# A linear-attention and GLU block on one core: squares of four more x tiles on ScalarE, their rows loaded earlier, and a new order

## The chip, the cores and the metric
The kernel runs on one core of a Trainium2 chip. The core has a matrix engine (TensorE, PE in the profile), VectorE (DVE), ScalarE (ACT), GpSimd (POOL) and a queue that here only issues DMAs (SyncE, SP). The metric is the device time of one execution in microseconds. The kernel before takes 280.59 us, the median of three runs (280.55 to 281.14).

## The reference
```python
x = A_x                                            # 1 x 2048 x 640, bf16
h = x + A(layernorm(x))
out = h + B(layernorm(h))
# A: qkv = x @ wqkv, 32 heads of 20; pq = q @ w_phi, pk = k @ w_phi (20 x 20 a head)
phi_q = concat(softmax(pq), softmax(-pq))          # 40 features a head, phi_k likewise
kv = phi_k^T v ;  z = sum over the sequence of phi_k
o = (phi_q kv) / (phi_q z + 1e-6) ;  A = o @ wo
# B: (x @ w_gate) * (x @ w_up) @ w_down            # 640 -> 1536 -> 640
```

## The kernel before
The 2048 rows of x are 16 tiles of 128. The 640 columns are five chunks of 128. PSUM is cut into four buffers of two banks each; nearly every step on TensorE takes one buffer and holds it until another engine has read it.

**The stages.** First the weights are prepared: `w_phi` is spread into a block-diagonal band `Phi` (masked by `G`, on VectorE for chunks 0 to 2, on GpSimd for 3 and 4), and the query and key parts of `wqkv` are turned, centred and multiplied by it, so that one matrix takes x straight to pq or pk. The key weights are turned on TensorE at the start (`wk_rounds`, units wk and x0 to x4). The query weights are loaded by the unit lwq, turned by DMAs (units t0 to t4), and centred row block by row block (`wq_means`: the means in unit wm, then units wq0 to wq4, line 739 on VectorE for 0, 2 and 4, line 736 on ScalarE for 1 and 3). The five rounds y0 to y4 (`wq_round`) then read all five centred blocks and write one chunk of the final weights each. The value weights are centred by units c0 to c4 after their sums (unit wv).

Then come the layer-norm statistics of x, in five batches (`stats`, units s0, s2, s4, s8, s12; the last three of four tiles). In the form with `act` false TensorE multiplies each transposed tile by itself and a column of ones (129 columns), and VectorE takes the diagonal by a product with the identity (line 617). In the form with `act` true, chosen by `ST_ACT`, TensorE multiplies by one column of ones only, and ScalarE squares the rows of x as they lie in `x_all` and sums them (`act_sum`, line 565). On GpSimd a chain of five to seven small operations makes 1/std from them (lines 622 to 633).

For each tile t there are a key step (k: ten matmuls of 320 columns; VectorE's largest absolute value, line 820, and its product `nb`, line 823; two exponentials on ScalarE, line 827), its normalisation (K: VectorE's sum over each head, line 838, and reciprocal, line 840; GpSimd's product of 1280 columns, line 841), a value step (v: ten matmuls, one scaled copy on ScalarE) and a query step (q and Q, like k and K but with lines 860 to 871). When the keys are done, sixteen steps A0 to A14 build kv in one PSUM buffer, and VectorE copies it, masked, to `KVsb` (line 907). Then, per block of four tiles, come the attention output (n), its projection (h), the gate and up products (f, named by block, chunk and first tile) and the down product (d, e).

**What sets the order.** Each operation belongs to a unit. `ORDER` holds for each engine a list of unit names; the n-th mention of a name is the n-th operation of that unit on that engine. Each engine runs strictly by its list. Semaphore waits follow from the data; a planner (`place`) with an assumed duration `t` for each operation only decides which of several equal buffers an operation takes. An `at` of a load is an assumed landing time for the same planner. All transposing DMAs of x (units lT4 to lT15, and four inside "in") and plain loads stand on SP's list, and at most eight transposing DMAs are under way.

`ones`, `ident`, `G`, `Gk`, the column of ones behind each x tile (`R_xone`) and ones columns of `vaug` are written by GpSimd at the start, in the order of the code.

Of the kernel before, what the change touches and what calls it, by code (L numbers as in the profile page):

```python
# [7 lines left out]
ACT = mybir.ActivationFunctionType  # L8
# [3 lines left out]
P = 128  # L12
S = 2048
D = 640
NT = S // P
NC = D // P
H = 32
DH = 20
# [11 lines left out]
DF = 2 * DH  # L30
NQ = 2 * NC
HQ = [P * c // DF for c in range(NQ)]
SL = 4
# [8 lines left out]
SC = 175.0 / 128.0  # L42
# [6 lines left out]

BATCH = [(0, 2), (2, 2), (4, 4), (8, 4), (12, 4)]  # L50

ST_ACT = (12,)

# [1 line left out]

ORDER = {
# [14 lines left out]
    "DVE":  # L73
# [12 lines left out]
    "ACT":  # L86
# [9 lines left out]
    "POOL":  # L96
# [10 lines left out]
}  # L107
# [270 lines left out]
def _build(ctx, nc, A_x, A_wqkv, A_w_phi, A_wo, B_w_gate, B_w_up, B_w_down, out):  # L378
    g = Prog(nc, ctx)
# [9 lines left out]
    xT = sb([P, NT, NC, XW], BF16, "xT")  # L389
# [8 lines left out]
    Wrows = sb([P, NC, DH], BF16, "Wrows")  # L398
    G = sb([P, NC, H], BF16, "G")
    Gk = sb([P, NC, SL], BF16, "Gk")  # L400
# [17 lines left out]
    mhalf = sb([P, 1], FP32, "mhalf")  # L418
    mone = sb([P, 1], FP32, "mone")
# [32 lines left out]
    R_Wnat, R_WT, R_Phi = regs(NC), [regs(NC), regs((NRAW + 1) * NC)], regs(NC)  # L452
# [13 lines left out]
    def load(out_, in_, wr, mb, eng="SP", at=0.0):  # L466
        return g.op(eng, lambda e: e.dma_start(out_, in_), wr=wr, dma=("w", 8), t=0.5, lat=0.4 if at else 1.9, size=mb / 0.38, at=at)  # L467
# [45 lines left out]

    U("in")
    load_wnat(1, (3, 5), "ACT", at=4.3)
    load(Wrows[:, :, :], A_w_phi.rearrange("h d f -> (h d) f").rearrange("(a p) f -> p a f", p=P), [R_Wrows], 0.03, eng="ACT", at=5.5)
    load_wnat(1, (0, 1), at=2.9)
    load_wnat(1, (1, 3), at=5.05)
    load_xT(0, 5.35)
# [6 lines left out]
    def pool_op(f, t, **k):  # L526
        return g.op("POOL", f, t=t, **k)
# [6 lines left out]

    def affine(reg, out_, pattern, base, mult):
        pool_op(lambda e: e.affine_select(out=out_, in_=out_, compare_op=ALU.is_ge, fill=0.0,
                                          base=base, pattern=pattern, channel_multiplier=mult), 0.17, rd=[reg], wr=[reg])

    pool_op(lambda e: e.memset(G[:, :, :], 1.0), 0.23, wr=R_G)
    for c in range(NC):  # L540
        affine(R_G[c], G[:, c, :], [[-DH, H]], P * c, 1)
    for c in range(NC):
        affine(R_G[c], G[:, c, :], [[DH, H]], DH - 1 - P * c, -1)
    pool_op(lambda e: e.memset(Gk[:, :, :], 1.0), 0.15, wr=[R_Gk])
    affine(R_Gk, Gk[:, :, :], [[P - 3 * DF, NC], [-DF, SL]], 0, 1)
    affine(R_Gk, Gk[:, :, :], [[3 * DF - P, NC], [DF, SL]], DF - 1, -1)
    for a in range(NC):
        lo, hi = CH[a]
        n = hi - lo + 1

        def phi_op(e, a=a, lo=lo, hi=hi, n=n):
            return e.tensor_tensor(out=Phi[:, a, 0:DH * n].rearrange("p (h f) -> p h f", f=DH),  # L552
                                   in0=Wrows[:, a, :].unsqueeze(1).to_broadcast([P, n, DH]),
                                   in1=G[:, a, lo:hi + 1].unsqueeze(2).to_broadcast([P, n, DH]), op=ALU.mult)
        g.op("DVE" if a < 3 else "POOL", phi_op, t=0.22 if a < 3 else 0.45, rd=[R_Wrows, R_G[a]], wr=[R_Phi[a]])
    pool_op(lambda e: e.memset(xT[:, :, :, P:P + 1], SC / D), 0.25, wr=[R_xone])
    pool_op(lambda e: e.memset(mhalf[:, :], -0.5), 0.1, wr=[R_const])
    pool_op(lambda e: e.memset(mone[:, :], -1.0), 0.1, app=[R_const])
    for b4 in range(NB):
        pool_op(lambda e, b4=b4: e.memset(vaug[:, 4 * b4:4 * b4 + 4, :, DH:E21], 1.0), 0.6, wr=R_vaug[4 * b4:4 * b4 + 4])  # L560

# [556 lines left out]
```

## Time and profile before
| | |
|---|---|
| median of the runs | 280.59 us |
| the profiled execution | 280.5 us |
| its span | 278.8 us |
| PE busy | 273.6 us |
| DVE busy | 166.2 us |
| ACT busy | 135.3 us |
| POOL busy | 107.3 us |
| granted TensorE clock | 0.999 |

In a row of the timeline the first number is the start in microseconds from the span's start, the second the time that the merged group took, then engine, line, operation, output and inputs, shape and count; in brackets stands the idle time before it and what ended it. Spans of neighbouring instructions on one engine overlap by up to a tenth of a microsecond, and for TensorE by more, so that a step is read from start to start. In a row of groups, the busy time and the mean in nanoseconds of one instruction stand behind the bar. In a row of waits the numbers are the total, the count and, where there is a third, the longest. Time between landing and issue of a DMA is the last number of its row. The profile shows lines of the kernel; operations in helpers such as `mms` (line 572) all carry one line.

### The profile page before, as it was taken

How to read it: one execution, taken by the hardware profiler on the slowest of the kernel's cores; microseconds unless marked ns; L12 is line 12 of the kernel's file. 1: busy time of each engine (PE TensorE's matmuls, PEld its weight loads, DVE VectorE, ACT ScalarE, POOL GpSimd, SP SyncE). 2: the span in 40 equal slices, each digit the busy share in tenths (PEclk: the TensorE clock that was granted, in tenths of full speed). 3: DMA queues.
4: the chain of work that ended last, by engine and by line, in shares of the span. 5: the costliest groups of instructions: out<-in, count | busy, mean ns of one | idle time of the engine just before them, and what ended most of it. 6: DMA issues, size and time to landing. Idle time of an engine off the chain costs nothing.

```text
span 278.8 us, 5485 instructions
## 1 busy us (share of the span) xinstructions
PE 273.6 (98%) x2227; PEld 186.8 (67%) x2239; DVE 166.2 (60%) x314; ACT 135.3 (49%) x229; POOL 107.3 (38%) x158
## 2 busy tenths in 40 slices
PE   8999999999999999999999999999999999999995
PEld 8777777778878788877656555776454444447773
DVE  1999999999999976578445745413250223324011
ACT  3469989999657455323664423113254314340132
POOL 6446799999732240061230912241200000250152
PEclk9999999999999999999999999999999999999999
DMA  7998984068165549558644031447312000000112
GB/s 198 274 143 185 126 275 156 6 151 316 26 73 119 96 93 290 138 94 211 74 101 91 24 70 28 118 94 96 94 27 23 0 0 2 0 24 26 47 47 71
DMA packets 65192, 28.06 MB, mean 101 GB/s; under 512 B 55696, under 2 KB 63888, under 8 KB 65168
## 3 DMA queue, kind: packets, MB, share of 16 engines
q1 hardware_dynamic: 64240, 27.37, 43.7%
q10 hardware_dynamic: 928, 0.35, 0.5%
q8 instruction: 17, 0.28, 0.5%
q14 instruction: 7, 0.06, 0.1%
HBM read 11.82 MB, written 2.62 MB: 52 GB/s over the span
## 4 chain that ended last, share of the span: by engine, by line
PE 95%; DMA 2%; DVE 1%; issue 0%; SPq 0%
PE ps L572 95%; DMA phiqT<-in_A_wqkv_dram 2%; PE ps L482 0%; DVE outb L1024 0%; DVE phiqT L717 0%; PE ps L661 0%; DVE Phi L552 0%; DVE KVsb L907 0%; SPq L467 0%; DVE nmean L690 0%; DVE KVsb L910 0%; DVE sm L613 0%; DVE nb L823 0%
## 5 line engine op out<-in xcount | busy, mean ns | idle before, releaser
L572 PE MATMUL ps<-phik,Wgu 128*128 128x512 bf16 (+1 forms) x589 | 105.9, 336 | 0.6
L572 PEld LDWEIGHTS ps<-phik,Wgu 128*128 128x128 bf16 x600 | 58.2, 98 | 43.5 <-DVE phik L983 1.8
L572 PE MATMUL ps<-Wp,xT 128*128 128x320 bf16 x480 | 68.6, 299 | 0.0
L983 DVE TENSOR_TENSOR phik<-ps,gate 128x512 bf16<-128x512 f32 (+1 forms) x60 | 33.8, 575 | 56.0 <-PE ps L572 51.2
L572 PE MATMUL ps<-vaug,phik 128*128 128x320 bf16 (+3 forms) x543 | 59.8, 270 | 0.1
L981 ACT ACTIVATE gate<-ps 128x512 bf16<-128x512 f32 (+1 forms) x60 | 29.8, 511 | 58.8 <-PE ps L572 43.3
L572 PEld LDWEIGHTS ps<-Wp,xT 128*128 128x128 bf16 x480 | 46.0, 98 | 17.9 <-ACT phik L827 0.5
L572 PEld LDWEIGHTS ps<-vaug,phik 128*128 128x128 bf16 x544 | 43.6, 97 | 15.6
L999 POOL TENSOR_TENSOR outb<-t,x_all 128x640 bf16<-128x640 f32 x12 | 16.8, 1396 | 58.0 <-ACT t L996 49.9
L841 POOL TENSOR_TENSOR phik<-phik,Rk 128x1280 bf16<-128x1280 bf16 x16 | 37.6, 2364 | 2.3 <-DVE Rk L840 2.0
L996 ACT ACTIVATE t<-ps,mh,rs 128x640 f32<-128x640 f32 x12 | 10.6, 883 | 37.8 <-PE ps L572 37.8
L820 DVE TENSOR_REDUCE ps<-ps 128x1 f32<-128x640 f32 x32 | 26.2, 818 | 1.5 <-PE ps L572 1.0
L860 DVE TENSOR_REDUCE Sq<-eq 128x64 f32<-128x1280 bf16 x16 | 23.6, 1473 | 2.7 <-ACT eq L827 2.7
L827 ACT ACTIVATE eq<-ps,nb,rs 128x640 bf16<-128x640 f32 x16 | 14.2, 885 | 20.2 <-DVE nb L823 12.3
L966 POOL TENSOR_SCALAR vpe<-shc 128x1 f32<-128x1 f32 x16 | 3.0, 190 | 52.9 <-ACT junk L565 51.9
L838 DVE TENSOR_REDUCE Ssum<-phik 128x64 f32<-128x1280 bf16 x16 | 23.4, 1471 | 0.0
L871 POOL TENSOR_TENSOR eq<-eq,rq 128x640 bf16<-128x640 bf16 x16 | 20.2, 1269 | 0.8
L866 POOL TENSOR_TENSOR rq<-Sq,rq 128x32 f32<-128x32 f32 x16 | 4.0, 254 | 39.9 <-DVE rq L865 39.9
L565 ACT ACTIVATE junk<-x_all 128x640 bf16<-128x640 bf16 x20 | 14.6, 732 | 4.4 <-DVE x_all L960 4.4
L827 ACT ACTIVATE phik<-ps,nb,rs 128x640 bf16<-128x640 f32 x16 | 14.1, 884 | 2.6 <-DVE nb L823 1.9
L941 DVE RECIPROCAL rden<-ps 128x32 f32<-128x32 f32 (+1 forms) x18 | 5.6, 323 | 14.6 <-PE ps L572 14.6
L827 ACT ACTIVATE phik<-ps,nb,nrs 128x640 bf16<-128x640 f32 x16 | 14.2, 885 | 0.0
(86 smaller groups left out, 245.1 us busy)
## 6 DMA issues: line engine op xcount, KB each, us to landing
x_all<-in_A_x_dram SPq DMA_DIRECT2D x4, 640.0 KB, 5.5
out_dram<-outb SPq DMA_DIRECT2D x15, 160.0 KB, 1.8
Wgu<-in_B_w_up_dram SPq DMA_DIRECT2D x1, 1920.0 KB, 7.9
Wgu<-in_B_w_gate_dram SPq DMA_DIRECT2D x1, 1920.0 KB, 10.2
vaug<-in_B_w_down_dram SPq DMA_DIRECT2D x1, 1920.0 KB, 8.6
Wp<-in_A_wqkv_dram SPq DMA_DIRECT2D x1, 800.0 KB, 5.0
phiqT<-in_A_wqkv_dram SPq DMA_DIRECT2D x1, 800.0 KB, 6.3
Wo<-in_A_wo_dram SPq DMA_DIRECT2D x1, 800.0 KB, 9.5
```

Source lines behind the costliest of these rows:

```text
L565: g.op("ACT", lambda e: e.activation(out=junk[:, v.i, :], in_=in_, func=func, accum_out=acc), rd=rd, wr=wr, use=[v], t=0.73, lat=0.97)
L572: ins = e.matmul(o_, lhsT=l_, rhs=r_, start=s_, stop=p_, skip_group_check=True)
L820: g.op("DVE", lambda e: e.tensor_reduce(out=mx(), in_=PS[v.i][:, :, 0:HALF], axis=AX.XY, op=ALU.max, apply_absolute_value=True, negate=Tru ...
L827: g.op("ACT", lambda e, s=s, sc=sc: e.activation(out=signed(dst(), s), in_=PS[v.i][:, :, 0:HALF].rearrange("p b (h f) -> p b h f", f=DH), ...
L838: g.op("DVE", lambda e: e.tensor_reduce(out=Ssum[:, vs.i, :], in_=x, axis=AX.X, op=ALU.add), rd=R_phik[t], wr=vs.R, use=[vs], t=1.39, lat=1.5)
L841: g.op("POOL", lambda e: e.tensor_tensor(out=x, in0=x, in1=Rk[:, vr.i, :].unsqueeze(2).to_broadcast([P, 2 * H, DH]), op=ALU.mult), rd=vr.R ...
L860: g.op("DVE", lambda e: e.tensor_reduce(out=Sq[:, vs.i, :], in_=eq[:, b.i, :].rearrange("p (g f) -> p g f", f=DH), axis=AX.X, op=ALU.add), ...
L871: return e.tensor_tensor(out=x, in0=x, in1=rq[:, vr.i, :].unsqueeze(2).to_broadcast([P, H, DH]), op=ALU.mult)
L981: g.op("ACT", lambda e: e.activation(out=gate[:, vg.i, 0:P * n], in_=PS[v.i][:, 0, 0:P * n], func=ACT.Copy), rd=[v.R[0]], wr=vg.R, use=[v, ...
L983: g.op("DVE", lambda e: e.tensor_tensor(out=hhT[:, hb, ft, sl], in0=PS[v.i][:, 1, 0:P * n], in1=gate[:, vg.i, 0:P * n], op=ALU.mult), rd=[ ...
L996: g.op("ACT", lambda e: e.activation(out=t32[:, v3.i, :].rearrange("p (b n) -> p b n", b=2), in_=PS[v.i][:, :, 0:HALF], func=ACT.Identity, ...
L999: g.op("POOL", lambda e: e.tensor_tensor(out=outb[:, vo.i, :], in0=t32[:, v3.i, :], in1=x_all[:, t, :], op=ALU.add), rd=v3.R + [R_h[t]], w ...
```

## The change
- `ST_ACT` becomes (8, 12): tiles 8 to 11 take the form with squares on ScalarE. Their rows (`x_all`, unit lx2, 640 KB) move on SP from the middle of the kernel to the first place behind the loads of unit "in", which end with transposed tiles 2 and 3 (tiles 0 to 3).
- On GpSimd the column of ones behind each x tile, and the two small constants, are written earlier, the column ahead of `G`. The ten selects that shape `G` by chunks of 32 columns become two over all 160 columns.
- The lists of all five engines are new up to the middle of the first GLU block; from "f0.5.0 n7" on they are the same but for single names. On SP the query weights go behind tiles 4, 6, 5, 10 and 7, both GLU weights are loaded ahead of Wo, where one of them came later. On TensorE keys and values of more tiles come ahead of the rounds y and the queries q.
- Some of the planner's durations differ. They do no work on the chip, beyond the choice of buffers.

```diff
-ST_ACT = (12,)
+ST_ACT = (8, 12)
 "PE":
-  warm wk*9 s0 wk s0 x1 x1 x3 wv wv x2 x0 x0 s2 s2 x4 k0*5 k3 k2 wm k1 v1 s4*4
-  k6 k4 v5 v0 k7 y3 v7 v4 y1 k5 y2 y4 s8 s8 s8 y0 s8 v2 v3 q0 q1 s12*4 k8 k10 v6 ...
+  warm wk*9 s0 wk x1 s0 x1 x3 wv wv x2 x0 x0 s2 s2 x4 k0*5 k2 k1 k3 v1 s4*4
+  v3 k5 v0 wm k4 v7 s8*4 k7 k6 v4 k8 v11 k9 y1 v10 y3 v8 s12*4 k11 y4 y2 k10 y0 ...
 "DVE":
-  ... k0 k0 c3 k3 k2 k3 K0 k2 k1 K3 k1 s4*5 wq2 k6 K3 k4 k6 K1 k4 wq0 K1 wq4 K0 k7 y3 ...
+  ... k0 k0 c4 k2 k1 k2 K0 k1 k3 K0 K2 s4 s4 s4 k3 s4 s4 K2 K1 k5 K1 k5 K3 k4 K5 s8 k4
+  wq0 k7 K3 K5 k7 k6 K4 k6 wq2 k8 wq4 k8 K7 y1 k9 K7 k9 y3 K8 s12 K4 K8 k11 ...
 "POOL":
-  in*20 wk s0 s0 s0 in in s0 in s0 s2 s0 s2 s2 in s2 s2 s2 in s4 s4 s4 s2 s4 s4 s4 K3 K1 in ...
+  in*14 wk s0*6 in s2 in s2*5 in K0 s4 s4 s4 s4 s0 s4 s4 in K1 s2 K2 s8*5 K5 s8 K3 K7 K4 ...
 "SP":
-  in*7 lwq lT6 lT5 lT4 t2 lT7 t3 t1 t0 t4 lx3 lT11 lT10 lT8 lT9 lT15 lT14 lT12 lT13 lu lwo ...
+  in*7 lx2 lT4 lT6 lT5 lT10 lT7 lwq lT8 t3 lT9 lT11 t0 t1 lT13 t2 t4 lx3 lT15 lT12 lT14 lg lu lwo ...
...
+    pool_op(lambda e: e.memset(xT[:, :, :, P:P + 1], SC / D), 0.45, wr=[R_xone])
     pool_op(lambda e: e.memset(G[:, :, :], 1.0), 0.23, wr=R_G)
-    for c in range(NC):
-        affine(R_G[c], G[:, c, :], [[-DH, H]], P * c, 1)
-    for c in range(NC):
-        affine(R_G[c], G[:, c, :], [[DH, H]], DH - 1 - P * c, -1)
+    affine(R_G, G[:, :, :], [[P, NC], [-DH, H]], 0, 1)
+    affine(R_G, G[:, :, :], [[-P, NC], [DH, H]], DH - 1, -1)
...
+    pool_op(lambda e: e.memset(mhalf[:, :], -0.5), 0.1, wr=[R_const])
+    pool_op(lambda e: e.memset(mone[:, :], -1.0), 0.1, app=[R_const])
...
-    pool_op(lambda e: e.memset(xT[:, :, :, P:P + 1], SC / D), 0.25, wr=[R_xone])
-    pool_op(lambda e: e.memset(mhalf[:, :], -0.5), 0.1, wr=[R_const])
-    pool_op(lambda e: e.memset(mone[:, :], -1.0), 0.1, app=[R_const])
```
(A name with a star and a number stands for that many mentions.)

More of the change, by code (lines that the diff above doesn't have):

```diff
@@ L515, in _build @@
     load_wnat(1, (3, 5), "ACT", at=4.3)
-    load(Wrows[:, :, :], A_w_phi.rearrange("h d f -> (h d) f").rearrange("(a p) f -> p a f", p=P), [R_Wrows], 0.03, eng="ACT", at=5.5)
+    load(Wrows[:, :, :], A_w_phi.rearrange("h d f -> (h d) f").rearrange("(a p) f -> p a f", p=P), [R_Wrows], 0.03, eng="ACT", at=5.35)
     load_wnat(1, (0, 1), at=2.9)
@@ L536, in affine @@
         pool_op(lambda e: e.affine_select(out=out_, in_=out_, compare_op=ALU.is_ge, fill=0.0,
-                                          base=base, pattern=pattern, channel_multiplier=mult), 0.17, rd=[reg], wr=[reg])
+                                          base=base, pattern=pattern, channel_multiplier=mult), 0.3, rd=reg, wr=reg)
+    pool_op(lambda e: e.memset(xT[:, :, :, P:P + 1], SC / D), 0.45, wr=[R_xone])
     pool_op(lambda e: e.memset(G[:, :, :], 1.0), 0.23, wr=R_G)
-    for c in range(NC):
-        affine(R_G[c], G[:, c, :], [[-DH, H]], P * c, 1)
-    for c in range(NC):
-        affine(R_G[c], G[:, c, :], [[DH, H]], DH - 1 - P * c, -1)
+    affine(R_G, G[:, :, :], [[P, NC], [-DH, H]], 0, 1)
+    affine(R_G, G[:, :, :], [[-P, NC], [DH, H]], DH - 1, -1)
     pool_op(lambda e: e.memset(Gk[:, :, :], 1.0), 0.15, wr=[R_Gk])
-    affine(R_Gk, Gk[:, :, :], [[P - 3 * DF, NC], [-DF, SL]], 0, 1)
-    affine(R_Gk, Gk[:, :, :], [[3 * DF - P, NC], [DF, SL]], DF - 1, -1)
+    affine([R_Gk], Gk[:, :, :], [[P - 3 * DF, NC], [-DF, SL]], 0, 1)
+    affine([R_Gk], Gk[:, :, :], [[3 * DF - P, NC], [DF, SL]], DF - 1, -1)
+    pool_op(lambda e: e.memset(mhalf[:, :], -0.5), 0.1, wr=[R_const])
+    pool_op(lambda e: e.memset(mone[:, :], -1.0), 0.1, app=[R_const])
     for a in range(NC):
@@ L554, in phi_op @@
                                    in1=G[:, a, lo:hi + 1].unsqueeze(2).to_broadcast([P, n, DH]), op=ALU.mult)
-        g.op("DVE" if a < 3 else "POOL", phi_op, t=0.22 if a < 3 else 0.45, rd=[R_Wrows, R_G[a]], wr=[R_Phi[a]])
-    pool_op(lambda e: e.memset(xT[:, :, :, P:P + 1], SC / D), 0.25, wr=[R_xone])
-    pool_op(lambda e: e.memset(mhalf[:, :], -0.5), 0.1, wr=[R_const])
-    pool_op(lambda e: e.memset(mone[:, :], -1.0), 0.1, app=[R_const])
+        g.op("DVE" if a < 3 else "POOL", phi_op, t=0.42, rd=[R_Wrows, R_G[a]], wr=[R_Phi[a]])
     for b4 in range(NB):
```

82 rows, old and new, of the table ORDER are left out of this document.

## The prediction
> **What bounds the kernel now.** I read the page first, for the engines' shares and the chain that ended last; then the busy time of each engine between 10 and 74 us, where the change does its work; then the timelines of PE, DVE and POOL there.
>
> ```profile
> span 278.8 us, 5485 instructions
> ...
> PE 273.6 (98%) x2227; PEld 186.8 (67%) x2239; DVE 166.2 (60%) x314; ACT 135.3 (49%) x229; POOL 107.3 (38%) x158
> ...
> PE 95%; DMA 2%; DVE 1%; issue 0%; SPq 0%
> ```
> ```profile
> sum 64.00, PE 63.94 PEld 48.86 DVE 63.40 ACT 55.85 POOL 52.95; mean PE 21.31 PEld 16.29 DVE 21.13 ACT 18.62 POOL 17.65
> ```
> Over the whole span PE is the bound: 98% busy, 95% of the chain. The second row is the sum over 10 to 74 us (the key, value and first query projections): PE 63.94 of 64.00, but DVE 63.40 too. The two march in step, so in this stage a microsecond lost on DVE is soon lost on PE. After 97 us DVE has room and only PE counts; the orders from there to the end are the same in both kernels, so what the head gains or loses goes through to the end.
>
> **The change part by part.** *Statistics of tiles 8 to 11.* Twenty matmuls 129 columns wide become twenty of one column.
>
> ```profile
> 12.87 4.25 PE L572 MATMUL ps<-Wp,xT 128*128 128x320 bf16 x30
> ...
> 17.59 2.88 PE L572 MATMUL ps<-Wp,xT 128*128 128x320 bf16 x20
> 20.30 1.30 PE L572 MATMUL ps<-xT 128*128 128x129 bf16 x20
> 21.43 7.17 PE L572 MATMUL ps<-Wp,xT 128*128 128x320 bf16 x50
> ...
> 40.90 0.64 PE L572 MATMUL ps<-ones,xT 128*128 128x1 bf16 x20
> 41.40 18.77 PE L572 MATMUL ps<-Wp,xT 128*128 128x320 bf16 x137
> ```
> Start to start: 20.30 to 21.43 is 1.13 us for the wide form, 40.90 to 41.40 is 0.50 for the narrow. PE saves 0.63 us. (17.59 to 20.30 gives a projection: 2.71 / 2 = 1.36 us.) By the Trainium skill, "TensorE: Matmul & The Clock Gate", section "Back-to-back issue gap", 128-column pairs sustain about 81 ns and small ones about 25 ns, an estimate of 1.1 us saved; the trace shows 57 and 25 ns, and I keep 0.63. DVE loses four products with the identity (0.21 us each, 22.34 to 22.55 below), 0.85 us. ACT gains four squares of the form
>
> ```profile
> L565 ACT ACTIVATE junk<-x_all 128x640 bf16<-128x640 bf16 x20 | 14.6, 732 | 4.4 <-DVE x_all L960 4.4
> ```
> 0.73 us each, 2.9 us in all; ACT has 8 us of room in the stage (55.85 busy of 64).
>
> *The head.* The ones column no longer stands behind Wrows on POOL, and the ten head-mask selects become two larger ones; POOL then waits for Wrows all the same, so nothing of the selects shows, unless the two took over a microsecond more than the ten. PE's first steps can move up, to the next wait: the value weights.
>
> ```profile
> 4.38 0.58 SPq L467 DMA_DIRECT2D Wp<-in_A_wqkv_dram  x1
> ...
> 9.28 0.49 PE L572 MATMUL ps<-Phi,phiqT 128*128 128x140 bf16 x6
> 9.61 0.57 PE L572 MATMUL ps<-Wp,ones 128*128 128x320 bf16 x3
> ```
> ```profile
> Wp<-in_A_wqkv_dram SPq DMA_DIRECT2D x1, 800.0 KB, 5.0
> phiqT<-in_A_wqkv_dram SPq DMA_DIRECT2D x1, 800.0 KB, 6.3
> ...
> xT<-in_A_x_dram SPq DMA_TRANSPOSE x16, 4.7
> ```
> They land at 4.38 + 5.0 = 9.38, so the sums that start at 9.61 can start at about 9.42: 0.19 us gained, between 0 and 0.3.
>
> *The loads.* The x rows (640 KB) take the place on SP of the query weights (800 KB), which go behind five transposes. Issued near 7.6 and no slower than those 800 KB (6.3 us), the rows land by about 14; the first square runs near 17. Tile 7, fifth in line, is issued near 14 and lands near 19; PE wants it near 20.4. Query weights and their transposes land from about 21 to 30, and their first user (the means) runs near 24.8. All hidden, with 1 to 3 us of room. The two large GLU weights now load at 32 to 46 us, away from any waiting transpose, and Wo behind them, 15 us ahead of its first user: zero.
>
> *The order.* This decides. The centring of the transposed query weights (L739, wq0, wq2 and wq4 on DVE) moves.
>
> ```profile
> 22.34 0.28 DVE L617 CUSTOM_DVE_ANT_0 t<-ps,ident 128x128 f32<-128x128 f32 x1
> 22.55 0.08 DVE L617 DVE_READ_ACCUMULATOR2_ANT sxx<- 128x1 f32 x1
> 22.55 0.38 DVE L739 TENSOR_SCALAR phiqT<-phiqT,nmeanq 128x640 bf16<-128x640 bf16 x1
> ...
> 26.61 1.15 DVE L739 TENSOR_SCALAR phiqT<-phiqT,nmeanq 128x640 bf16<-128x640 bf16 x1
> 27.68 0.54 DVE L840 RECIPROCAL Rk<-Ssum 128x64 f32<-128x64 f32 x1
> 28.15 0.28 DVE L739 TENSOR_SCALAR phiqT<-phiqT,nmeanq 128x640 bf16<-128x640 bf16 x1
> ...
> 48.48 0.82 DVE L820 TENSOR_REDUCE ps<-ps 128x1 f32<-128x640 f32 x1
> 49.22 1.48 DVE L838 TENSOR_REDUCE Ssum<-phik 128x64 f32<-128x1280 bf16 x1
> 50.61 0.15 DVE L823 TENSOR_TENSOR nb<-ps,rs 128x1 f32<-128x1 f32 x1
> ```
> ```profile
> 22.72 0.30 POOL L623 TENSOR_SCALAR vpe<-sxx 128x4 f32<-128x4 f32 x1 [0.64 <-DVE sxx L617]
> ...
> 25.22 2.36 POOL L841 TENSOR_TENSOR phik<-phik,Rk 128x1280 bf16<-128x1280 bf16 x1
> 28.30 2.36 POOL L841 TENSOR_TENSOR phik<-phik,Rk 128x1280 bf16<-128x1280 bf16 x1 [0.72 <-DVE Rk L840]
> ```
> The same operation takes 0.28 us when POOL is idle (28.15; POOL starts at 28.30) and 1.15 us when POOL is multiplying keys: started at 26.61, it ends at 27.76, just after POOL's operation of 25.22 ends at 27.58. One stalled case could be read as a fixed slowing to 1.15 us or as a wait for POOL's end. The Trainium skill, "SBUF — State Buffer", section "SBUF: two separate sides", holds that DVE in a two-port mode and GpSimd exclude each other for a whole instruction, which is the second reading; by the first the three would cost at most 3.5 us together, hardly different from the sum below.
>
> Now where do they fall? Steps, start to start, from the rows: reduce 0.74, sum 1.40, reciprocal 0.47, nb 0.07 (an estimate, half its span). PE starts k0 0.19 us earlier than at 12.87 and feeds the key reduces at 1.36 us a projection: k1, third in the new order, is done at 12.68 + 3 × 1.36 = 16.8 and is reduced from 16.95 to 17.69. Then three sums (K0, K2, K1: 4.2), two reduces (k3, k5: 1.47), three reciprocals (1.4), the statistics of s4 (0.92) and nb's (0.2) follow: K1's reciprocal ends near 25.9. POOL takes K0 behind its reciprocal, from 20.6 to 23.0, then s4's chain (2.5 us, as from 22.72 to 25.22), and runs K1 from 26.0, a short operation and K2 from 28.6 to 30.9. On DVE behind K1's reciprocal stand nb, K3's sum, k4's reduce, K5's sum, s8's copy, nb: 3.76 us, then wq0 at 29.6. It meets K2 and ends at 31.1. Next come 3.9 us (k7, two reciprocals, k6, K4, nb's): wq2 at 35.0. POOL has run s8's chain (2.2 us, to 33.2) and is in K5 until 35.6: wq2 ends at 35.75. One reduce later, 36.5, wq4 meets K3 (35.75 to 38.1) and ends at 38.3. The three take 1.5 + 0.75 + 1.8 = 4.0 us, where the present kernel spends 1.8 (0.38, 1.15, 0.28). Bounds for the three: 0.85 (all free, as at 28.15) and 7.1 (each behind a full 2.36). I take 4.0, because the first follows K1's reciprocal by a count of DVE steps that ends inside K2, and each later one is then set by POOL's end.
>
> What waits behind them: round y1 on PE reads all five centred rows, so it starts at 38.4, where PE is free at 37.3 by the same walk (and v11 has waited 0.5 for k7's exponentials, delayed on DVE by wq0): with small waits for k8 (its nb is behind wq4), y3 and v8, PE stands still 2.0 us. PE ends s12 near 42.5 with 18 projections and two rounds behind it; the present kernel ends s12 at 41.40 with 17 and five. Put on the same work (1.36 − 3 × 0.32, a round being 9.28 to 9.61): 42.5 against 41.8, and 0.15 more at k11. So the new kernel is about 0.85 us late there. The other moves (keys ahead of queries, the first GLU units in another sequence) leave each engine the same operations; I put them at zero, give or take 0.3 us for a wait more or less. DVE agrees: from k11's reduce, near 45.6, to the first copy of KVsb stand twelve sums, ten reduces, eight reciprocals of keys, three of queries (taken as half as long, for half the columns) and ten nb's, 16.8 + 7.4 + 3.8 + 0.7 + 0.7 = 29.4 us, to 75.0; now it starts at
>
> ```profile
> 74.11 0.58 DVE L907 TENSOR_TENSOR KVsb<-ps,Gk 128x400 bf16<-128x400 f32 x1
> ```
> **The sum.** Against the profiled execution (span 278.8, 280.5 in all): −0.63 (matmuls) − 0.19 (head) − 0.3 (of the two PE gaps of the row below, which have other work in front of them in the new order; between 0 and 0.5) + 2.0 (PE standing still) = +0.9 us: 281.4. The median of the runs, 280.59, is 0.1 above the profiled one; I leave that out.
>
> ```profile
> PEld ps L572 <- ACT phik L827: 0.5, 2, 0.4
> ```
>
> **The rivals.** *The stalls are not there* (chance 0.20). If the three operations cost 0.3 to 0.6 each, the gains stand alone: 0.63 + 0.19 + 0.3 = 1.1 us, 279.4. For it: POOL's times are partly its own waits, and a shift of 1.3 us would put wq0 behind K2. Against: DVE and POOL are tied by K1's reciprocal, so they shift together. It decides from the point where the three together cost under about 3 us.
>
> *The stalls are absorbed* (0.12). The 4.0 us on DVE are there, but PE's four accumulators and the later slack take up half: the effect is nil, 280.5. For it: the order has other work in flight. Against: y1 stands in PE's own queue and holds all behind it.
>
> *A load is late* (0.08). Tile 7 behind the x rows, with 1 us of room, or the x rows before ACT's first square, behind which k2's exponentials stand. Each microsecond past the room is one on PE; 2 us more than the forecast: 283. Against: 800 KB stood in the same place before, and 640 stand there now.
>
> **How the numbers follow.** Forecast as walked: 0.60, 281.4, with its own range 280.8 to 282.3. What a measurement of this kernel can tell from no change is about 0.2%, 0.56 us: 280.03 to 281.15. The first rival is faster (0.20), the second mostly the same (0.09 same, 0.02 faster, 0.01 slower), the third slower (0.08); of the forecast 0.08 lies within the same band. Faster 0.22, same 0.17, slower 0.61. The range reaches from the first rival's 279.4 less a little to the forecast's upper end: 279.3 to 282.4.
>
> **What would show it.** Right: L737 (the same operation, two lines up) at about 1.5, 0.75 and 1.8 us, each ending just after a POOL multiply by Rk; a gap of a microsecond on PE ahead of y1's six 140-column matmuls near 38; s8 in 0.5 us on PE; the first KVsb copy near 75. Wrong: those operations at 0.3 to 0.4 us, or DVE arriving at wq0 when POOL is in short operations; then KVsb comes near 73. A wait of s4 or of ACT's first square on a DMA would speak for the late load.

## The result, and the profile after

The changed kernel takes 281.09 us (median of 16 runs, 280.96 to 283.29); the kernel before took 280.67 us beside it (16 runs, 280.47 to 281.14). The ratio is 1.0023, with a 95% interval of 1.0014 to 1.0032: slower, by 0.42 us between the medians. The forecast was 281.4 us. The times of the changed kernel fall in two groups, ten runs from 280.96 to 281.20 and five from 281.34 to 281.57, with one at 283.29. The profiled execution, at 281.36 us (span 279.6), belongs to the upper group, which matters further down. Of all runs in this document one alone, the slowest of experiment 1, counts as a slow run, and the ratio there leaves it out.

The page, and the sum row of the busy times from 10 to 74 us (the stage of the change), for the changed kernel:

```profile
span 279.6 us, 5495 instructions
...
PE 273.2 (98%) x2239; PEld 185.1 (66%) x2239; DVE 167.6 (60%) x306; ACT 137.9 (49%) x237; POOL 106.8 (38%) x150
...
PE 82%; DVE 6%; DMA 5%; ACT 3%; SPq 2%; issue 1%; POOL 1%
```
```profile
sum 64.00, PE 62.85 PEld 47.08 DVE 63.30 ACT 57.23 POOL 53.27; mean PE 20.95 PEld 15.69 DVE 21.10 ACT 19.08 POOL 17.76
```

PE is still the bound, but its share of the chain falls from 95% to 82%, and in the stage it is busy for 62.85 of 64 us where it was busy for 63.94: it now stands still for 1.15 us. VectorE is as full as it was (63.30 against 63.40), although it does four products with the identity less. Its timeline says what filled it. These are the three centrings of query weights (wq0, wq2, wq4), and below them POOL's products of a key tile with its reciprocal sums (start, duration):

```profile
29.50 1.58 DVE L737 TENSOR_SCALAR phiqT<-phiqT,nmeanq 128x640 bf16<-128x640 bf16 x1
...
34.81 0.77 DVE L737 TENSOR_SCALAR phiqT<-phiqT,nmeanq 128x640 bf16<-128x640 bf16 x1
...
36.24 1.98 DVE L737 TENSOR_SCALAR phiqT<-phiqT,nmeanq 128x640 bf16<-128x640 bf16 x1
```
```profile
28.55 2.36 POOL L839 TENSOR_TENSOR phik<-phik,Rk 128x1280 bf16<-128x1280 bf16 x1
...
33.04 2.36 POOL L839 TENSOR_TENSOR phik<-phik,Rk 128x1280 bf16<-128x1280 bf16 x1
...
35.68 2.35 POOL L839 TENSOR_TENSOR phik<-phik,Rk 128x1280 bf16<-128x1280 bf16 x1
```

Add start and duration. The centrings end at 31.08, 35.58 and 38.22; POOL's products end at 30.91, 35.40 and 38.03. Each centring ends 0.17 to 0.19 us behind a POOL product, wherever it began, and so did the one held centring of the kernel before (27.76, behind 27.58). Together they take 4.33 us, where the kernel before spent 1.81. Not every VectorE operation is held: the sum over a key tile takes 1.47 us inside a POOL product and 1.47 us with POOL idle (started at 33.35 and at 38.21).

PE's timeline in that place, and what held it, in the same kernel:

```profile
28.18 0.64 PE L570 MATMUL ps<-ones,xT 128*128 128x1 bf16 x20
28.69 5.59 PE L570 MATMUL ps<-Wp,xT 128*128 128x320 bf16 x40
34.46 2.89 PE L570 MATMUL ps<-Wp,xT 128*128 128x320 bf16 x20 [0.18 <-ACT phik L825]
38.27 0.49 PE L570 MATMUL ps<-Phi,phiqT 128*128 128x140 bf16 x6 [0.92 <-DVE nb L821]
...
40.03 0.49 PE L570 MATMUL ps<-Phi,phiqT 128*128 128x140 bf16 x6
40.47 1.53 PE L570 MATMUL ps<-Wp,xT 128*128 128x320 bf16 x10
41.83 0.64 PE L570 MATMUL ps<-ones,xT 128*128 128x1 bf16 x20
42.40 1.53 PE L570 MATMUL ps<-Wp,xT 128*128 128x320 bf16 x10
```
```profile
PEld ps L570 <- DVE phiqT L737: 1.3, 1, 1.3
```

The statistics of tiles 8 to 11 take 0.51 us start to start (28.18 to 28.69), as forecast. Then PE waits 0.18 us for ScalarE ahead of v11, and 0.92 us ahead of y1 at 38.27. The row of PE names the bias of k8 as the releaser; the row of waits of its weight loads names L737, the third centring, which ended at 38.22. Both became free within a tenth of a microsecond.

Two later places, in rows of VectorE, PE and SP:

```profile
74.64 0.57 DVE L905 TENSOR_TENSOR KVsb<-ps,Gk 128x400 bf16<-128x400 f32 x1
...
117.96 0.82 DVE L941 TENSOR_TENSOR ob<-ps,rden 128x640 bf16<-128x640 f32 x1 [0.90 <-DMA vaug<-ob]
```
```profile
75.42 0.56 PE L570 MATMUL ps<-KVsb,phiqT 128*128 128x84 bf16 x10
76.34 0.56 PE L570 MATMUL ps<-KVsb,phiqT 128*128 128x84 bf16 x10 [0.37 <-DVE KVsb L908]
...
118.84 1.53 PE L570 MATMUL ps<-Wp,xT 128*128 128x320 bf16 x10 [0.28 <-DVE ob L941]
```
```profile
108.35 0.58 SPq L467 DMA_DIRECT2D vaug<-in_B_w_down_dram  x1
```

The kernel before has the first use of KVsb at 74.89, its second at 75.66, and the projection of the last row at 117.92. So the changed kernel is 0.53 us late at the first, 0.68 at the second and 0.92 at the last. One step ahead of the last it is only 0.47 late (117.30 for 116.83). The other 0.45, of which the profile shows 0.28 as idle time of PE, I had not forecast: W_down's load goes out at 108.35 (103.98 before), the transposes of the attention output behind it on SP land late, VectorE waits 0.90 us for them before it writes `ob` again, and PE waits for VectorE, which is still reading the accumulator that this projection takes.

### The profile page after: what moved, and what is told of

Its sections match the earlier page's. It is cut to its first block, busy times and chain, and to the rows that moved or that the text cites. A ratio compares the mean times of both kernels' runs of the same rounds, so it can differ in the third digit from the quotient of the medians.

```text
span 279.6 us, 5495 instructions
## 1 busy us (share of the span) xinstructions
PE 273.2 (98%) x2239; PEld 185.1 (66%) x2239; DVE 167.6 (60%) x306; ACT 137.9 (49%) x237; POOL 106.8 (38%) x150
## 4 chain that ended last, share of the span: by engine, by line
PE 82%; DVE 6%; DMA 5%; ACT 3%; SPq 2%; issue 1%; POOL 1%
PE ps L570 81%; DMA vaug<-ob 3%; ACT phik L825 2%; DMA phiqT<-in_A_wqkv_dram 2%; SPq L471 1%; DVE phiqT L737 1%; DVE ps L818 1%; DVE Ssum L836 1%; ACT vaug L845 1%; ACT junk L563 1%; DVE Sq L858 0%; POOL eq L869 0%; PE ps L659 0%; PE ps L482 0%; DVE phiqT L715 0%
## 5 line engine op out<-in xcount | busy, mean ns | idle before, releaser
L570 PE MATMUL ps<-phik,Wgu 128*128 128x512 bf16 (+1 forms) x600 | 107.5, 336 | 0.0
L563 ACT ACTIVATE junk<-x_all 128x640 bf16<-128x640 bf16 x24 | 17.6, 734 | 4.4 <-DVE x_all L958 4.4
L958 DVE SCALAR_TENSOR_TENSOR x_all<-ps,mh,x_all 128x640 bf16<-128x640 f32 x16 | 14.0, 876 | 0.4
```

The costliest lines, as they stand in the source:

```text
L563: g.op("ACT", lambda e: e.activation(out=junk[:, v.i, :], in_=in_, func=func, accum_out=acc), rd=rd, wr=wr, use=[v], t=0.73, lat=0.97)
L570: ins = e.matmul(o_, lhsT=l_, rhs=r_, start=s_, stop=p_, skip_group_check=True)
L958: g.op("DVE", lambda e: e.scalar_tensor_tensor(out=xv, in0=PS[v.i][:, :, 0:HALF], scalar=mh[:, t:t + 1], in1=xv, op0=ALU.subtract, op1=ALU ...
```

## The experiments

Ten kernels were run. Differences below are between a kernel's median and the median of the kernel before that ran beside it (280.65 for experiments 1 to 4, 280.50 for 5 to 8, 280.67 for 9 and 10), so that they can be compared with the change's +0.42. Lines of these kernels' rows are four lower than those of the changed kernel (the centring is L733, the projection L566), three lower than those of the kernel before in experiments 2 and 3 (L736, L569), and six lower in experiment 4.

**The theory:** PE stands still because the centrings wait on VectorE until POOL's products end. **Rivals:** the centrings' place in the order matters, but through the transposes that they wait for; ScalarE or the early x rows are the loss; the second place, near 118 us, is the loss.

### 1. The centrings in POOL's short chain

```diff
 "DVE" of the changed kernel:
-  K5 s8 k4 wq0 k7 K3 K5 k7 k6 K4 k6 wq2 k8 wq4 k8
+  K5 s8 k4 k7 wq0 wq2 wq4 K3 K5 k7 k6 K4 k6 k8 k8
```

> The changed kernel with one edit on VectorE's list: wq0, wq2 and wq4 come together behind k7's reduce, when GpSimd is in the short operations of s8's chain (30.9 to 33 us in the profile of the changed kernel). Theory (the three stalls behind GpSimd's products make the loss): each of the three takes 0.3 to 0.4 us, the PE gap ahead of y1 near 38 us is gone, and the time falls by 1.5 to 2.0 us, to 279.1 to 279.6. Rival (the new order itself fills the accumulators, and the stalls are only where it shows): the operations are short but PE waits elsewhere, 280.8 to 281.3.

Measured: 282.04 us, spread over 279.88 to 284.46 (12 runs); ratio 1.0043 (1.001 to 1.0075). Neither time that I had expected came. VectorE, one group and one row, and PE:

```profile
L733 DVE TENSOR_SCALAR phiqT<-phiqT,nmeanq x3: 386/387/441, 31.2 to 34.1; 128x640 bf16<-128x640 bf16 x3
```
```profile
34.09 0.39 DVE L733 TENSOR_SCALAR phiqT<-phiqT,nmeanq 128x640 bf16<-128x640 bf16 x1 [2.07 <-DMA phiqT<-in_A_wqkv_dram]
```
```profile
37.13 2.89 PE L566 MATMUL ps<-Wp,xT 128*128 128x320 bf16 x20 [2.60 <-ACT phik L821]
```

The group's three numbers are minimum, median and maximum in nanoseconds: away from POOL's products the same three operations take 0.39 to 0.44 us, not 0.77 to 1.98. The wait for POOL is gone, but a new wait has taken its place: wq4 stands 2.07 us for the transpose of its weights, everything behind it on VectorE stands too, and PE loses 2.60 us. The late order had hidden that landing. The fastest run, 279.88, may be what is left when the transpose lands in time; experiment 8 tests that.

### 2. A stall put into the kernel before

```diff
 "DVE" of the kernel before:
-  K1 wq4 K0 k7 y3
+  K1 K0 wq4 k7 y3
```

> The kernel before with one edit on VectorE's list: wq4, which ran in 0.28 us with GpSimd idle, comes one reciprocal later, when GpSimd has begun the next product by Rk (28.3 to 30.7 us). Theory (VectorE waits for the end of GpSimd's product): wq4 takes 2.0 to 2.3 us, round y3 on PE starts near 30.9 in place of 28.5, and the time rises by 1.5 to 2.2 us, to 282.1 to 282.8. Rival (a fixed slowing to 1.15 us): rises by 0.8 to 1.2. Rival (the length of these operations does not matter to the end): within 0.2.

Measured: 285.28 us (4 runs, 285.12 to 286.44); ratio 1.0171 (1.0155 to 1.0188). VectorE, POOL and PE of this kernel, then windows of one microsecond (start:end, length, then busy us of PE, weight loads, VectorE, ScalarE, POOL; the third number from the end is the granted clock):

```profile
28.78 2.88 DVE L736 TENSOR_SCALAR phiqT<-phiqT,nmeanq 128x640 bf16<-128x640 bf16 x1
```
```profile
28.53 2.35 POOL L838 TENSOR_TENSOR phik<-phik,Rk 128x1280 bf16<-128x1280 bf16 x1 [0.72 <-DVE Rk L837]
30.82 0.66 POOL L557 MEMSET vaug<- 128x128 bf16 x1
```
```profile
31.72 0.49 PE L569 MATMUL ps<-Phi,phiqT 128*128 128x140 bf16 x6 [2.89 <-DVE phiqT L736]
32.05 4.56 PE L569 MATMUL ps<-Wp,xT 128*128 128x320 bf16 x20
36.44 0.48 PE L569 MATMUL ps<-Phi,phiqT 128*128 128x140 bf16 x6
```
```profile
32.00:33.00 1.00, 1.00 (x10) 0.62 (x7) 1.00 (x2) 0.00 (x0) 1.00 (x1) 0.62 0.64 129
33.00:34.00 1.00, 1.00 (x6) 0.52 (x5) 1.00 (x3) 0.00 (x0) 0.87 (x1) 0.50 0.82 151
34.00:35.00 1.00, 1.00 (x5) 0.57 (x4) 1.00 (x2) 0.24 (x1) 0.00 (x0) 0.50 0.67 150
35.00:36.00 1.00, 1.00 (x6) 0.63 (x5) 0.97 (x1) 1.00 (x2) 0.00 (x0) 0.67 0.43 55
```

One step back in VectorE's list costs 4.6 us. The operation that took 0.28 us at 28.15 in the kernel before now starts at 28.78, a quarter of a microsecond behind the start of POOL's product, and takes 2.88: to 31.66. That is 0.78 behind the product's end (30.88) and 0.18 behind the end of the MEMSET that follows it (31.48); it seems to have waited for both, in this one case. POOL's next product, right behind the MEMSET, took 2.78 us (from 31.09), and the one behind the MEMSET in the kernel before 2.46: about the length of one centring more, as if that product had waited in its turn. All this is more than my expectation, which reckoned with the first product alone, and the time rose by 4.6 us where I had expected 1.5 to 2.2. PE waits 2.89 us. The second surprise is in the rows after: the 20 matmuls at 32.05 take 4.39 us to the next start, where the same 20 take 2.72 in the kernel before:

```profile
28.81 2.88 PE L572 MATMUL ps<-Wp,xT 128*128 128x320 bf16 x20
31.53 0.48 PE L572 MATMUL ps<-Phi,phiqT 128*128 128x140 bf16 x6
```

The granted clock fell to 0.50 right after the standstill. 2.89 and 1.67 make 4.56, the whole loss.

### 3. The squares alone, in the kernel before

```diff
-ST_ACT = (12,)
+ST_ACT = (8, 12)
 "ACT":
-  x4 k0 k0 wm k3 ... y2 y4 y0 v2
+  x4 s8 s8 k0 k0 s8 wm k3 ... y2 y4 y0 s8 v2
 "DVE":
-  K4 s8 k5 s8 K7 s8 s8 s8 q0
+  K4 s8 k5 K7 q0
 "SP":
-  lwq lT6 lT5 lT4 ... (lx2 in the middle of the kernel)
+  lx2 lwq lT6 lT5 lT4 ...
```

> The kernel before with the part of the change that concerns the squares alone: tiles 8 to 11 squared on ScalarE, their rows loaded ahead of the query weights, four squares put into ScalarE's idle time (two ahead of k0's exponentials, one behind them, one ahead of v2), and the four products with the identity off VectorE's list; else the old order. Theory: PE's 0.63 us show in full, 280.0 to 280.2. Rival (the earlier rows make the transposed tiles 6, 5, 4 and the query weights late): a wait on PE at s4 near 20 us or at y3, 281 or more.

Measured: 281.13 us (280.75 to 281.75, 11 runs); ratio 1.0017 (1.0009 to 1.0026). The forecast missed. PE:

```profile
21.77 0.46 PE L569 MATMUL ps<-xT 128*128 128x129 bf16 x5 [0.23 <-DMA xT<-in_A_x_dram]
...
34.65 0.51 PE L569 MATMUL ps<-ones,xT 128*128 128x1 bf16 x15
35.39 0.49 PE L569 MATMUL ps<-Phi,phiqT 128*128 128x140 bf16 x6 [0.23 <-ACT Wp L765]
```

With the rows ahead of the query weights and of all four tiles, the last tile of the group 4 to 7 lands late (PE waits 0.23 us for it), and y0 then waits 0.23 us for ScalarE. The extra square is not what holds ScalarE there: it stands behind y0 in its list, and up to there ScalarE runs the list that it had, 0.63 us later, as PE is (the square of tile 12 at 33.90 for 33.27, y2 on PE at 33.83 for 33.20). The narrow s8 only brings PE to y0 sooner than ScalarE has copied out the rounds in front of it. From start to start the statistics of tiles 4 to 7 are 1.53 us long for 1.13 (20.53 to 22.06), a loss of 0.40, and y2 to the end of s8 is 2.16 for 2.27 (33.83 to 35.99), a gain of 0.11 in place of 0.63. That makes 0.29 of the measured 0.48; the rest I have not found. So the rival "a load is late" is true in the old order, and ScalarE hides most of the gain besides. In the changed kernel the query weights stand behind five tiles instead, and no such wait is there. So the squares cannot be had by that edit alone; what they are worth is measured in experiment 9.

### 4. The head alone, in the kernel before

```diff
 "PE":
-  s0 wk s0 x1 x1 x3
+  s0 wk x1 s0 x1 x3
 "DVE": the three operations on Phi together, the second and third s0 one place earlier
 "POOL": the two selects in place of ten, the ones column and the constants first
```

> The kernel before with the head of the change alone: column of ones and constants first on GpSimd, two selects on G in place of ten, the three Phi operations of VectorE together, x1 ahead of the second s0 on PE. Theory: the sums of the value weights start at 9.4 in place of 9.6 us and the time falls by 0.1 to 0.3 us, 280.4 to 280.6. Rival (DVE, busy without a gap after it, keeps the pace): no change, within 0.1.

Measured: 280.43 us (280.26 to 280.60, 11 runs), 0.22 under the kernel before; ratio 0.9990 (0.9981 to 0.9999). PE:

```profile
9.38 1.52 PE L566 MATMUL ps<-Wp,ones 128*128 128x320 bf16 x10
```

The sums over the value weights start at 9.38 in place of 9.61. The prediction had 9.42, but by the landing of the weights; here they are there in time (issued at 4.4, 4.9 us to land), and PE comes straight from the step before. One profile is thin ground for 0.23 us: with the new head the sums start between 9.29 and 9.59 in seven other profiles, and at 10.55 in that of experiment 9, with the old head at 9.84 in those of experiments 2 and 3. The two groups do not overlap but for the late landing, and the medians agree, with an interval from almost nothing to 0.5 us.

### 5. One centring on ScalarE, two in the short chain

```diff
-            if a in (1, 3):
+            if a in (1, 3, 4):
 "DVE" of the changed kernel:
-  K5 s8 k4 wq0 k7 K3 K5 k7 k6 K4 k6 wq2 k8 wq4 k8
+  K5 s8 k4 k7 wq0 wq2 k7 K3 K5 k6 K4 k6 k8 k8
 "ACT":
-  k7 k7 v4 k6 k6 v11
+  k7 k7 v4 k6 k6 wq4 v11
```

> The changed kernel with the three centring operations taken out of the reach of POOL's products: wq0 and wq2 stand on VectorE right behind k7's row maximum (where POOL is in the short statistics chain, 31.1 to 33.2 us), and wq4 is done by ScalarE behind k6's two exponentials, where ScalarE had idle time before 38.32 us. The theory (the lock made PE stand still) gives: wq0 and wq2 at 0.39 each; wq4 on ScalarE about 0.9 from 36.4 to 37.4, so that the landing of its transpose near 34 us is out of play too; PE has no wait of 0.92 ahead of y1, which starts at 37.4 to 37.6 in place of 38.27; about 1.0 us less than the changed kernel's 281.09, so 280.0 to 280.3, with a small spread. First rival (the landing of the fifth transpose is what counts, not the lock): wq4 still late, times spread over several us as in the first experiment. Second rival (ScalarE becomes the bound): its 0.77 us pushes v11 and k8's exponentials, PE waits on ScalarE, and the time stays within 0.3 us of 281.1.

Measured: 280.14 us (280.02 to 281.01, 11 runs), 0.36 under the kernel before; ratio 0.9990 (0.9981 to 0.9999). VectorE, ScalarE and PE:

```profile
31.11 0.74 DVE L733 TENSOR_SCALAR phiqT<-phiqT,nmeanq 128x640 bf16<-128x640 bf16 x2
```
```profile
36.51 0.82 ACT L730 ACTIVATE phiqT<-phiqT,nmeanq 128x640 bf16<-128x640 bf16 x1
```
```profile
37.39 0.49 PE L566 MATMUL ps<-Phi,phiqT 128*128 128x140 bf16 x6 [0.27 <-ACT phiqT L730]
```

y1 starts at 37.39, 0.88 earlier than in the changed kernel, and the kernel is 0.8 us faster than the changed one (−0.36 against +0.42). ScalarE does its centring in 0.82 us although POOL's product runs from 35.75 to 38.10: the wait is one of VectorE, not of every engine that reads that memory. Of the rivals, neither shows here: the times are not spread by a landing, and ScalarE did not become the bound.

### 6. The divisions of query tiles 8 and 4 earlier

```diff
 "DVE" of the changed kernel:
-  Q4 Q8 f0.0.0 f0.6.0 q10 Q8 f0.9.0 n7 q10 n7 f0.10.2 f0.5.0 Q4
+  Q4 Q8 f0.0.0 Q8 f0.6.0 Q4 q10 f0.9.0 n7 q10 n7 f0.10.2 f0.5.0
```

> The changed kernel with one edit at 98 to 103 us: the division steps of query tiles 8 and 4 on VectorE stand one and two GLU units earlier (directly behind the first and the second gated product that follow the two sums), as the two last query tiles stood in the kernel before. The theory of the second place: query tile 4's product on POOL ends near 101.5 in place of 104.3, the W_down load is issued near 105.5 in place of 108.35, and the transposes of the attention output behind it land before PE wants them at 117.9: the wait of 0.28 us behind the attention output near 118.8 is gone, the time is 280.6 to 280.8 (0.3 to 0.5 less), and the upper group of times (281.3 to 281.6) disappears. Rival (the transposes are held by the load that shares the DMA queue, whenever it starts): the wait stays, 281.1, and the two groups stay.

Measured: 281.12 us (281.06 to 281.56, 11 runs); ratio 1.0021 (1.0012 to 1.0030). SP and PE:

```profile
104.74 0.58 SPq L463 DMA_DIRECT2D vaug<-in_B_w_down_dram  x1
```
```profile
118.65 1.52 PE L566 MATMUL ps<-Wp,xT 128*128 128x320 bf16 x10
```

The edit did what it should: the load goes out 3.6 us earlier, and the wait of 0.28 us is gone. The median did not move. The likely reading is that the wait near 118 us belongs to the profiled execution, which was one of the upper group, and not to the typical one: the two groups of the changed kernel lie 0.45 us apart by their medians (281.05 and 281.50), just what the wait costs start to start. No profile of a run of the lower group was taken, so this is not shown, and the edit may also cost something elsewhere: in this profile PE is 0.26 us later than in the changed kernel's ahead of the place (117.56 for 117.30). Only one of 11 runs is above 281.3 here, against six of 16 for the changed kernel; that agrees with a wait that some executions have, but is too little to prove it.

### 7. Both edits

> Both edits together: the centring operations out of the lock, and the divisions of query tiles 8 and 4 earlier. If the two places are independent and all of the loss, the gains add: about 279.5 to 279.9, which is the kernel before less the gains of the change (0.63 of matmuls, 0.2 to 0.3 of the head) and a remainder of small waits. If the second place only matters because PE comes late, or PE comes earlier now and waits more at 118 us, the sum is less: 280.0 to 280.3.

Measured: 280.19 us (280.01 to 280.39, 11 runs); ratio 0.9987 (0.9978 to 0.9996). Experiment 5 gave 280.14 on the same chip: the second edit adds nothing on top of the first.

### 8. Experiment 1 with the fifth transpose early

```diff
 "DVE" as in experiment 1
 "SP":
-  lwq lT8 t3 lT9 lT11 t0 t1 lT13 t2 t4 lx3
+  lwq lT8 t3 lT9 lT11 t0 t4 t2 t1 lT13 lx3
```

> The first experiment again (wq0, wq2 and wq4 on VectorE behind k7's row maximum), with the transpose of the fifth block of query weights issued third among the five, ahead of the first, second and x tile 13, so some 5 us earlier. If the landing of that transpose made the first experiment slow and wide (279.9 to 284.5, wq4 waiting 2.07 us), wq4 now runs at 0.39 directly behind wq2, near 32.5, PE has no wait of 2.6 ahead of its next projection, and the time is 279.9 to 280.3 with a spread below 1 us; the first experiment's fastest run, 279.88, is the mark. If instead three centrings in a row on VectorE delay the exponentials (0.39 us each in front of k7's bias), PE still loses 0.5 or more: 280.6 to 281.2. If another of the transposes is now the late one, the times stay wide.

Measured: 279.85 us (279.69 to 279.90, 7 runs), 0.65 under the kernel before; ratio 0.9971 (0.9961 to 0.9982). VectorE and PE:

```profile
30.92 1.04 DVE L733 TENSOR_SCALAR phiqT<-phiqT,nmeanq 128x640 bf16<-128x640 bf16 x3
```
```profile
34.62 2.89 PE L566 MATMUL ps<-Wp,xT 128*128 128x320 bf16 x20 [0.40 <-ACT phik L821]
37.34 0.48 PE L566 MATMUL ps<-Phi,phiqT 128*128 128x140 bf16 x6
```

All three centrings take 1.04 us together, in a row, where the changed kernel spends 4.33. The spread of 4.6 us in experiment 1 shrinks to 0.2: it was the landing. This kernel is faster than both kernels of the study.

### 9. The squares undone, in experiment 8's kernel

```diff
-ST_ACT = (8, 12)
+ST_ACT = (12,)
 "DVE":
-  K5 s8 k4 k7 wq0
+  K5 s8 k4 s8 s8 s8 s8 k7 wq0
 "ACT": without its four s8
```

> The eighth experiment's kernel (centrings in POOL's short chain, fifth transpose early) with one part of the change undone: the squares of x tiles 8 to 11 go back to the product of x with itself on TensorE and four reductions on VectorE (0.21 us apart), which stand behind k4's bias, where VectorE has waited 0.65 us for PE. The step of the prediction that priced the squares at 0.63 us of matmuls (20 of 64 ns against 20 of 32) says: s8 on PE takes 1.28 in place of 0.64, VectorE hides its four reductions in that wait, and the time is 0.63 above the eighth experiment's: about 280.5. Rival: ScalarE's four squares (4 x 0.72) and their rows cost something elsewhere that goes away, so that the difference is under 0.3: 279.8 to 280.1. Second rival: the four reductions delay k7's maximum and the centrings meet POOL's next product, so the loss is over 1 us: 281 or more.

Measured: 280.56 us (280.30 to 282.15, 12 runs), 0.11 under the kernel before; ratio 1.0001 (0.9979 to 1.0023). Against experiment 8, each to its own kernel before, that is 0.54 us more. PE of this kernel, then of experiment 8:

```profile
29.50 1.30 PE L566 MATMUL ps<-xT 128*128 128x129 bf16 x20
30.64 5.60 PE L566 MATMUL ps<-Wp,xT 128*128 128x320 bf16 x40
```
```profile
28.12 0.64 PE L566 MATMUL ps<-ones,xT 128*128 128x1 bf16 x20
28.63 5.59 PE L566 MATMUL ps<-Wp,xT 128*128 128x320 bf16 x40
```

Start to start the wide form takes 1.14 us and the narrow one 0.51: 0.63 on PE. That the first profile is 1.38 later there has for the most part another cause: its run took 281.67 us, the value weights landed late, and PE stood 1.01 us for them at 10.55. The time agrees with the 0.63, but loosely, since the interval of this experiment is 0.6 us to each side. Against experiment 10, on the same chip, it is 0.53: eleven of that kernel's twelve runs lie at 280.29 or below, all of this one's at 280.30 or above. So the squares on ScalarE are worth about what the matmuls say, once nothing else stands in the way.

### 10. The bias of k7 ahead of two divisions

```diff
 "DVE" of experiment 8:
-  wq0 wq2 wq4 K3 K5 k7 k6 K4 k6 k8 k8
+  wq0 wq2 wq4 k7 K3 K5 k6 K4 k6 k8 k8
```

> The eighth experiment's kernel with one more edit on VectorE: k7's bias stands right behind the three centrings, ahead of the two divisions (0.95 us) that stood between. In the eighth experiment ScalarE stood still 0.64 us for that bias and PE 0.40 us for ScalarE ahead of the projection at 34.62. Theory: both waits go, PE gains up to 0.4, the time is 279.45 to 279.6 in place of 279.85. Rival: the divisions now come 0.1 us later, POOL's two products with them, and the next centring or key waits: no gain, 279.8 to 280.0.

Measured: 280.03 us (279.70 to 281.69, 12 runs), 0.64 under the kernel before; ratio 0.9973 (0.9952 to 0.9994). No gain over experiment 8 (0.65). PE:

```profile
37.01 0.48 PE L566 MATMUL ps<-Phi,phiqT 128*128 128x140 bf16 x6
37.63 1.53 PE L566 MATMUL ps<-Wp,xT 128*128 128x320 bf16 x10
39.00 0.48 PE L566 MATMUL ps<-Phi,phiqT 128*128 128x140 bf16 x6
```

The wait of 0.40 us is gone and y1 starts 0.33 us earlier (37.01 for 37.34), but the next projection follows 0.62 us behind it, where experiment 8 needs 0.32 (37.34 to 37.66): most of the wait has moved one step on, and y3 starts at 39.00 in the one and 39.02 in the other. The two profiles do not start level, though: in this one the sums over the value weights start 0.24 us later (9.53 for 9.29), and so does s8 (28.36 for 28.12). Counted from s8, y3 comes 0.26 us earlier. So the edit may have gained up to 0.26 us in this stage; the times, with an interval of 0.6 us to each side, cannot tell that from the rival's nothing.

## Why the prediction was right, and which of its sizes were off

The sign and the mechanism were right, the size of the largest term was not, and that the sign came out was in part luck. By the prediction's own words a change under 0.56 us could not be told from none; the measured 0.42 lies inside that, at 281.09 in its band of 280.03 to 281.15, and only the narrow interval of 16 runs makes it a loss.

- *The order decides, by the centrings.* Right in nearly every number: forecast starts 29.6, 35.0 and 36.5 (measured 29.50, 34.81, 36.24), forecast durations 1.5, 0.75 and 1.8 (1.58, 0.77, 1.98), y1 at 38.4 (38.27), s12 done near 42.5 (42.40), the first KVsb copy near 75.0 (74.64). Experiments 5 and 8 take the wait away in two ways and both gain; experiment 2 puts it into the kernel before and loses. The first rival, no stalls, is ruled out by the three durations. The Trainium skill, "SBUF — State Buffer", section "Who interferes with whom", says that VectorE in a two-port mode and GpSimd exclude each other for a whole instruction, and that ScalarE waits for neither. The runs agree, for VectorE waiting on POOL and for ScalarE: ends 0.17 to 0.19 us behind POOL's end, and ScalarE's centring at 0.82 us inside a POOL product; which mode VectorE was in, no run shows. They also decide between the two readings that the prediction left open: a fixed slowing to 1.15 us does not give 0.77, 1.98 and 2.88.
- *PE stands still for 2.0 us.* This is the mis-sized term. PE waited 0.18 and 0.92, 1.10 us in all. VectorE lost 2.5 us (4.33 for 1.81) and PE about half of that, much as the second rival had it, which let half of the stalls be absorbed. The 0.92 ahead of y1 is close to the forecast (38.4 less 37.3); the 0.5 for v11 was 0.18, and most of the small waits for k8, y3 and v8 that I had added were not there: 40.03 to 40.47 is 0.12 above a round's 0.32, and 41.83 to 42.40 is 0.07 above s12's 0.50. Experiment 8, without that standstill, is 1.07 us better than the changed kernel (−0.65 against +0.42), the same size, though 0.40 us of another wait is left in its profile.
- *The squares, −0.63.* Measured 0.62 on PE (1.13 before, 0.51 after), and in time about 0.5, loosely (0.54 between experiments 8 and 9, 0.53 between 10 and 9); in the old order ScalarE hid all of it but 0.11 (experiment 3).
- *The head, −0.19.* Measured −0.22 in experiment 4; in the changed kernel the sums over the value weights start at 9.35 in place of 9.61, and there they do wait for the landing, as forecast:

```profile
9.35 1.53 PE L570 MATMUL ps<-Wp,ones 128*128 128x320 bf16 x10
```

- *Two old gaps on PE, −0.3.* Wrong. Gaps of that size came back in other places: 28.69 to 34.46 is 5.77 us for four projections of 1.36, 0.33 too much, of which the listed wait explains 0.18.
- *The loads are hidden.* Right in the changed kernel: no wait of s4 or of a square on a DMA. But the room was thinner than the prediction said: with the query weights still ahead of the tiles (experiment 3) tile 7 is late, and with wq4 some 4 us earlier (experiment 1) the fifth transpose is; it lands near 34 there, where the prediction had all of them by about 30.
- *After 97 us only PE counts.* Half right. The W_down load did go out 4.4 us later and cost the profiled run 0.45 us, which I had not seen in the diff: the division of query tile 4 stands some places later in VectorE's list. Experiment 6 removes it and leaves the median where it was, so it is probably no part of the median.

With the measured terms: −0.54 (squares) − 0.22 (head) + 1.07 (standstill) = +0.31, against +0.42 measured. The 1.07 is itself taken from the +0.42, so the sum tests one thing alone: the two gains make 0.76, and experiment 8, which has them without the standstill, shows 0.65. The 0.1 between them is within what these medians can tell. The forecast of +0.9 had one term too large by 0.9 and one gain of 0.3 that was not there. The two errors partly cancelled: with PE's real standstill of 1.1 and the 0.3, the prediction's own sum would have been −0.63 − 0.19 − 0.3 + 1.1, which is nil.

## What to carry to other kernels

Some VectorE operations, here the bf16 centring from memory to memory, are priced by what POOL does when they start, not by their size (0.28 to 2.88 us for the same work), while the sums beside them are not: look up POOL's row at that moment before moving one. When such an operation is moved earlier, look for the next thing it waits for (here a transpose), and move that too, or the new wait takes the old one's place. One profiled execution can show a wait that the median does not have; compare its own time with the other runs before giving the wait a price, and see that two profiles start level before comparing a time in one with a time in the other.

## What the runs showed of the hardware

- A standstill of TensorE of 2.89 us was followed by four windows at a lower clock (0.62, 0.50, 0.50 and 0.67 from 32 to 36 us of experiment 2), which cost another 1.67 us. The shares missing in the four windows (0.38, 0.50, 0.50 and 0.33) make 1.71 us, an estimate that agrees with it. In the profile of experiment 1 a standstill of 2.60 us was followed by no such drop: 20 matmuls in 2.72 us (37.13 to 39.85). Its runs of 283.2 us and above show a mean granted clock of 0.994, as experiment 2's profile does, those of 282.2 and below 0.999 or 1.000. The Trainium skill, "TensorE: Matmul & The Clock Gate", section "Why this matters for your kernels", advises against gaps of more than about 3 us; here one of 2.89 us was already enough. Whether its length or the moment at which it fell made the difference to the 2.60 us, two profiles cannot show.
- A small POOL MEMSET (0.66 us) that followed a POOL product seems to have held VectorE's centring too: it ended 0.18 us behind the MEMSET's end in experiment 2.
- The spread of a kernel's times can be a landing time: 4.6 us of spread in experiment 1 became 0.2 us in experiment 8, by the order of transposes on SP.
